# Value-block differences moved from the attention of a batch to the feed-forward of the batch in front, and two late output stores moved two chunks forward

## The chip, the cores and the metric

The kernel runs on one core of a Trainium2 chip. The metric is the time of one execution on the device in microseconds (us); several executions are made and the median is taken. One core has a matrix engine (PE, with its weight loads shown as PEld), a vector engine (DVE), a scalar engine (ACT), a general engine (POOL) and a sync engine (SP). Each works through its own list of instructions in order, and waits for the others through semaphores. DMAs are issued from such a list too: an issue that has to wait, or that takes time itself, holds up whatever stands behind it in the same list. In this kernel nearly all DMAs are issued from SP and POOL.

## The reference

Per batch (8 batches, 3008 tokens, 256 channels, 64 query/key dimensions) a gated attention without softmax, and then a feed-forward over all 24064 tokens:

```python
scores = (z @ z.T) / S                      # 3008 x 3008, symmetric
attn   = relu(scores) ** 2
x      = u * (attn @ v)                     # 3008 x 256
h      = x @ w_in                           # 256 -> 2048
out    = (h * sigmoid(1.702 * h)) @ w_out   # 2048 -> 256
```

Everything is computed in 16-bit floats with 32-bit accumulation; input and output are 32-bit.

## The kernel before, in words

**Tiling.** A batch is cut into 6 chunks of 512 tokens (the last has 448); a chunk has 4 blocks of 128 tokens, so a batch has 24 blocks, the last one half full. Because the score matrix is symmetric, only a part of it is computed: a unit (i, jp) is the pair of key blocks 2jp and 2jp+1 against the queries of chunk i. `scores` (L242) makes it on PE, `relu` (L261) takes it out of PSUM on ACT into one of 3 `rl` buffers, `square` (L270) squares it on DVE into a tile `a`. The mirrored part is made by transposing: `turn_unit` (L326, issue at L331) and two lines of `square` (L287 for the tile `ad` on the diagonal, L308 for `al`) issue DMA transposes from SP. Four of them fill two tiles, `TT[b, i, cj]`.

**Attention of a batch.** Chunks 0, 1, 2 and 5 go through `attend` (L634): per step a few matmuls of value blocks against weights, 24 or 48 steps a chunk, with the gate by `u` on DVE at the end of the chunk (L694). From batch 1 on, chunks 3 (`attend_rows`, L533) and 4 (`attend_split`, L483) are done by Strassen-like products with seven instead of eight parts (P1 to P7). These need sums and differences of the score tiles (`score_forms`, tiles `sa`, L430 to L448) and of the value blocks: `value_forms` (L371) makes four differences for each of three pairs of chunks t = 0, 1, 2, as one or two DVE instructions each (L384), into tiles `vt` of the ring `tt`, which has 14 buffers and is shared with `TT` and with the tiles `gt` of the feed-forward. `still` (L474) hands them to the matmuls of chunks 3 and 4. `VZ` is the half-full last value block, filled by a copy on POOL.

**Order.** All engines' lists are written out by hand. The main loop (L1113) goes over batches, chunks i and steps n; tables keyed by (i, n) say what is slipped in. `fills(b)` (L595) gives the DVE work of chunks 0 to 4: before the change the 12 value forms stand at chunk 0, steps 20 to 43, and chunk 1, steps 14 to 31; the score forms of chunk 3 stand at chunk 1 step 35 to chunk 3 step 18, those of chunk 4 at chunk 3 step 28 to chunk 4 step 23. `sched` says at which steps new units are taken. While chunk 5 runs, the units of chunk 0 of the next batch are made, and their transposes are kept in the list `late`.

**Feed-forward.** `up_group(b, q)` (L717), q = 0 to 47, makes two 128-column groups of `h` on PE (L732), the gelu on ACT (L745, 2 buffers `gf`), and the scaling to `gt` on DVE (L751) or, for q mod 8 in 1, 3, 5, on ACT (L749). The first 16 groups run inside chunk 4, the other 32 after chunk 5, each followed by one part of the second product (`pair_product`, L885; sums of `gt` on DVE, L858 to L871). The last 11 parts (12 for even batches) follow without up groups: the loop over `steps`, L1201, called the tail here. There P7, P3 and P2 are taken out of PSUM by DVE (L922), and P1, P5, P6 by ACT (L920); P7's accumulator is also P4's. From q = 44 on one entry of `late` is issued per step.

**Stores.** `store(b, k)` (L1002) transposes a finished 512-token block `Y[b, k]` on DVE into `yo` (L1007; one buffer) and issues the DMAs to the output from SP (L1017): 4 of 128 KB, or, for the last block of an odd batch, 12 smaller ones, because its last 64 tokens go to another place. Blocks 4 and 5 are not stored in the tail: they wait in `LAST2` and are stored in the attention of the next batch, before the change at chunk 3 step 4 and chunk 4 step 9 (L1144). `Y` has 2 buffers, and the staging tiles `zst` for the next batch's z share them.

**Loads in chunk 4.** At step 4 POOL copies two elements of `TT[b, 4, 5]` into `hold` (L1150), which makes its list wait for the last two transposes of chunk 3, and then issues the loads of the next batch's z (`stage_z`, L160, two halves). `twice_z` (L176) doubles each half on ACT (L179, at steps 19 and 28 of chunk 4) and transposes it from SP (L182). The loads of `u` for chunks 4 and 5 (L214) are on SP too.

Of the kernel before, what the change touches and what calls it, by code (L numbers as in the profile page):

```python
# [10 lines left out]
F16 = mybir.dt.float16  # L11
P = 128
# [3 lines left out]
def kernel(  # L16
# [20 lines left out]
    NJ = (S + P - 1) // P  # L37
# [333 lines left out]
    def value_forms(b, t):  # L371

        def form(f):
            if t not in VT:
                VT[t] = pa.tile([P, 4, CB, P], F16, name="vt", tag="tt", bufs=14)
            (k1, _, _), = key_half(b, t, 0)
            for k2, g, n in key_half(b, t, 1) if f else [(None, 0, CB)]:
                out_, t1, t2 = (VT[t][:, x, g:g + n] for x in (f, 0, 1))
                b11, b12 = k1[:, g:g + n, 0], k1[:, g:g + n, 1]
                a_, b_ = (  # L380
                    (b12, b11) if f == 0 else (k2[:, :, 1], t1) if f == 1
                    else (k2[:, :, 1], b12) if f == 2 else (k2[:, :, 0], t2)
                )
                dve.tensor_tensor(out_, a_, b_, ALU.subtract)  # L384

        return [lambda f=f: form(f) for f in (0, 2, 1, 3)]
# [87 lines left out]
    def still(b, t, g, name):  # L474

        if name in ("P1", "P2", "P3"):
            j = 8 * t + g + (0 if name == "P1" else CB)
            return channels(VZ if j == NJ - 1 else V16[b][:, j], int(name == "P3"))
        return VT[t][:, {"P5": 0, "P6": 1, "P7": 2, "P4": 3}[name], g]

    LAST_SPLIT = (("P2", (2,)), ("P7", (0, 1, 2)), ("P3", (0, 1, 2)), ("P4", (0, 1, 2)))

# [111 lines left out]

    def fills(b):  # L595

        VT.clear()
        SA.clear()
        at = {(0, 19): [lambda: pool.tensor_copy(VZ[TOP], V16[b][TOP, NJ - 1])]}

        def put(i, ns, ops):
            assert len(ns) == len(ops), (i, len(ns), len(ops))
            for n, op in zip(ns, ops):
                at.setdefault((i, n), []).append(op)

        near, far = NCH - 3, NCH - 2
        put(0, (20, 23, 26, 28, 34, 37, 40, 43), value_forms(b, 0) + value_forms(b, 1))
        put(1, (14, 20, 27, 31), value_forms(b, 2))
        put(1, (35, 38, 41, 44), score_forms(b, near, 0))
        put(2, (20, 21, 25, 26, 28, 31, 32), score_forms(b, near, 1, ("S1", "S2", "S3", "S4")))  # L610
        put(2, (38, 39), score_forms(b, near, 2, ("S3",)))
        put(3, (2, 2, 10, 11, 16, 18), score_forms(b, near, 2, ("S1", "S2", "S4")))
        if b < B - 1:
            put(3, (28, 30, 32, 37), score_forms(b, far, 0))
        else:
            put(2, (30, 41), score_forms(b, far, 0, ("S1", "S2")))
            put(3, (28, 30), score_forms(b, far, 0, ("S4", "S3")))
        if b == B - 1:
            put(3, (33, 36), score_forms(b, far, 1, ("S1", "S2")))
            put(4, (3, 5, 7, 9), score_forms(b, far, 2, ("S1", "S2")))  # L620
            put(4, (12, 14), score_forms(b, far, 1, ("S3", "S4")))
            put(4, (17, 19, 21, 23), score_forms(b, far, 2, ("S3", "S4")))
            return at
        put(4, (3, 5), score_forms(b, far, 1, ("S1", "S2")))
        put(4, (9, 10, 12, 13), score_forms(b, far, 2, ("S1", "S2")))
        put(4, (15, 20), score_forms(b, far, 1, ("S4", "S3")))
        put(4, (17, 18, 22, 23), score_forms(b, far, 2, ("S4", "S3")))
        return at
# [434 lines left out]
    LOADL = {(3, 36): 5}  # L1063
    TWICE = {19: 0, 28: 1}

    FIRST_ZT, FIRST_CAST = {12: 4, 20: 5}, {5: 4, 13: 5}
    SCHED0 = {
        0: {2: 1, 6: 2, 14: 2, 22: 2, 30: 2, 38: 2},
# [44 lines left out]
    for b in range(B):  # L1113
        nup = NCH * NFG
        more = b + 1 < B
        sched = SCHED0 if b == 0 else SCHED if more else SCHED_LAST
        turn, load = (TURN, LOAD) if b else (TURN0, LOAD0)
        if split(b, NCH - 2):
            turn, load = (TURNS, LOADS) if more else (TURNL, LOADL)
        head = 0  # L1120
        for i in range(NCH):
            host = b + 1 if more and i == NCH - 1 else b
            if host > b:
                fill(host)
                LATE.append(host)
            if i == 0 and split(b, NCH - 2):
                extra = fills(b)
            for n, step in enumerate(
                attend_split(b, i) if split(b, i) else attend_rows(b, i) if rowed(b, i)
                else attend(b, i, b == 0 and i == 0)  # L1130
            ):
                if b == 0 and i == 0 and n in (5, 24):
                    load_u(0, n // 24)
                if b == 0 and i == 0 and n == 2:
                    copies = first_zt(3)
                if b == 0 and i == 0 and n == 3:
                    copies()
                if b == 0 and i == 0 and n in FIRST_CAST:
                    first_cast(FIRST_CAST[n], True)
                if b == 0 and i == 0 and n in FIRST_ZT:  # L1140
                    first_zt(FIRST_ZT[n])()
                if (i, n) in turn:
                    turn_u(b, turn[i, n])
                if (i, n) in (((3, 4), (4, 9)) if more else ((5, 4), (5, 24))) and LAST2:  # L1144
                    LAST2.pop(0)()
                if (i, n) == (0, 22) and COPY:
                    COPY.pop(0)()
                if split(b, i) and more and n == 4:
                    hold = pw.tile([P, 2], F16, name="hold", tag="hold")
                    pool.tensor_copy(hold, TT[b, i, NCH - 1][:, ::2, 0, 0])  # L1150
                if (i, n) in load:
                    load_u(b, load[i, n])
                if b == 0 and (i, n) in CASTW:
                    cast_w(CASTW[i, n])
                if b == 0 and (i, n) in LOADW:
                    load_w(LOADW[i, n])
                if b == 0 and (i, n) == (NCH - 2, 6):
                    stage_z(1, 0, tag="yo", bufs=1)
                if more and (i, n) == (NCH - 2, 4 if b else 16):
                    load_z(b + 1)  # L1160
                if hosted(b) and i == NCH - 1 and n in LATESUMS:
                    some_sums(NCH * NFG)
                if more and split(b, i) and n in TWICE:
                    twice_z(b + 1, TWICE[n] * NU)
                if b == 0 and i == NCH - 1 and n in (8, 30, 42):
                    wsums.pop(0)()
                take(host, sched[i].get(n, 0))
                if split(b, NCH - 2):
                    for op in extra.get((i, n), ()):
                        op()  # L1170
                if split(b, i):
                    step()
                if i == full(b) and n >= HEAD and (n - HEAD) * LAGY // (2 * NJ - 10) >= head and head < LAGY:
                    up_group(b, head)
                    head += 1
                if not split(b, i):
                    step()
        late.sort(key=lambda t: t[0])
        if more:
            for i in range(2):  # L1180
                load_u(b + 1, i)
            for n0 in range(0, NJ, VB):
                load_v(b + 1, n0)
        prods = products(b)
        for q in range(head, nup):
            if more and q in (head + 14, head + 20):
                k = int(q == head + 20)
                turn_u(b + 1, k)
                load_u(b + 1, k + 2)
            up_group(b, q)  # L1190
            if b == 0 and q == head + 3:
                wsums.pop(0)()
            prods.pop(0)()
            for a_ in AFTER:
                a_[0] -= 1
            while AFTER and AFTER[0][0] < 0:
                AFTER.pop(0)[1]()
            if q >= 44 and late:
                late.pop(0)[1]()
        steps = prods  # L1200
        for step in steps:  # L1201
            step()
            for sum_ in [SUMS.pop(0) for _ in range(min(len(SUMS), 1 + (len(SUMS) > 4)))]:
                sum_[2]()
            for _, turn_it in [late.pop(0) for _ in range(min(len(late), 1 + (len(steps) < 10)))]:
                turn_it()
        LATE.clear()
        if b + 2 == B:
            load_u(b + 1, NCH - 2, "gf")
        if more:  # L1210
            while late:
                late.pop(0)[1]()
            take(b + 1, 2)
# [30 lines left out]
```

## Time and profile before

| | |
|---|---|
| median of 3 executions | 1164.87 us (1164.55 to 1165.69) |
| profiled execution: its own time / span of its instructions | 1164.78 us / 1162.9 us |
| granted PE clock | 1.00 in all 40 slices |
| busy, of the span | PE 99%, DVE 86%, ACT 78%, POOL 15% |
| value forms (L384), 7 batches | 105 DVE instructions, 59.1 us (26.6 + 26.6 + 3.9 + 2.0) |
| store transposes (L1007), all | 46 DVE instructions, 56.2 us |
| DMA issues: store of 128 KB | 156, 2.8 us to landing |
| DMA transposes `tt` / `ad` | 232, 3.4 us / 35, 2.5 us to landing |
| loads of z (192 KB) | 7, 6.3 us to landing |

The attention of batch 1 begins at about 158 us, that of the others at 302, 443, 588, 729, 873 and 1015 us. In batch 2, chunk 0 begins at 302, chunk 1 at 318, chunk 2 at 328, chunk 3 at 338 and chunk 4 at 348 us.

How to read it: busy times are sums over one execution. A timeline line gives the start, the time, the engine, the source line, the operation, what it writes and reads, how many instructions are merged in the line, and in brackets the idle time before it with what ended it. "SPq" and "POOLq" are the lists in which DMAs are issued; the time of an SPq line is the time that issuing took, not the transfer.

### The profile page before, as it was taken

How to read it: one execution, taken by the hardware profiler on the slowest of the kernel's cores; microseconds unless marked ns; L12 is line 12 of the kernel's file. 1: busy time of each engine (PE TensorE's matmuls, PEld its weight loads, DVE VectorE, ACT ScalarE, POOL GpSimd, SP SyncE). 2: the span in 40 equal slices, each digit the busy share in tenths (PEclk: the TensorE clock that was granted, in tenths of full speed). 3: DMA queues.
4: the chain of work that ended last, by engine and by line, in shares of the span. 5: the costliest groups of instructions: out<-in, count | busy, mean ns of one | idle time of the engine just before them, and what ended most of it. 6: DMA issues, size and time to landing. Idle time of an engine off the chain costs nothing.

```text
span 1162.9 us, 22852 instructions
## 1 busy us (share of the span) xinstructions
PE 1156.2 (99%) x8720; PEld 609.7 (52%) x8720; DVE 999.5 (86%) x1736; ACT 907.6 (78%) x1065; POOL 179.1 (15%) x248
## 2 busy tenths in 40 slices
PE   9999999999999999999999999999999999999998
PEld 3544456544465445654446545465444654547446
DVE  7789879998799987999879997899978999698876
ACT  7888867788678886688876887768868688684785
POOL 3033200132001320023100231003110131200000
PEclk9999999999999999999999999999999999999999
DMA  9996399754997559976498765996559874695123
GB/s 225 202 168 98 76 172 163 106 92 88 175 154 104 91 108 175 145 110 88 97 176 145 115 89 106 178 145 109 84 104 175 136 122 81 130 176 91 32 37 74
DMA packets 480543, 143.62 MB, mean 123 GB/s; under 512 B 447664, under 2 KB 476080, under 8 KB 480432
## 3 DMA queue, kind: packets, MB, share of 16 engines
q1 hardware_dynamic: 426272, 108.26, 55.3%
q0 software_dynamic: 52800, 32.58, 18.0%
q8 instruction: 68, 1.11, 0.4%
q10 hardware_dynamic: 1360, 1.31, 0.3%
q14 instruction: 43, 0.35, 0.1%
HBM read 60.29 MB, written 24.64 MB: 73 GB/s over the span
## 4 chain that ended last, share of the span: by engine, by line
PE 97%; DVE 1%; ACT 1%; issue 0%; SPq 0%; DMA 0%; DVEq 0%; ACTq 0%
PE o L677 29%; PE hg L732 27%; PE st L905 23%; PE sc L254 6%; PE oz L499 5%; PE oz L557 5%; PE st L953 1%; PE yp L879 1%; ACT rl L267 0%; PE w L101 0%; DMA uq<-in_u_dram 0%; SPq L308 0%; DVE gt L751 0%; ACT gf L745 0%; DVE yo L1007 0%
## 5 line engine op out<-in xcount | busy, mean ns | idle before, releaser
L745 ACT ACTIVATE gf<-hg 128x1024 f32<-128x1024 f32 (+1 forms) x384 | 382.3, 1003 | 85.9 <-PE hg L732 66.9
L267 ACT ACTIVATE rl<-sc 128x1024 f16<-128x1024 f32 (+1 forms) x344 | 310.6, 940 | 117.7 <-PE sc L254 104.3
L732 PE MATMUL hg<-xt,W 128*128 128x512 f16 (+1 forms) x1408 | 353.4, 374 | 0.1
L677 PE MATMUL o<-a,V 64*128 64x512 f16 (+3 forms) x2078 | 266.8, 368 | 0.3 <-DVE a L298 0.3
L751 DVE TENSOR_SCALAR gt<-gf 128x1024 f16<-128x1024 f32 x282 | 195.0, 694 | 64.0 <-ACT gf L745 61.9
L677 PEld LDWEIGHTS <-V 64*128 64x128 f16 (+1 forms) x3058 | 156.2, 94 | 172.1 <-issue 5.6
L732 PEld LDWEIGHTS <-W 128*128 128x128 f16 x1536 | 149.6, 98 | 156.4 <-issue 3.2
L298 DVE TENSOR_TENSOR a<-rl 128x1024 f16<-128x1024 f16 (+1 forms) x223 | 148.8, 673 | 49.2 <-ACT rl L267 48.6
L214 POOL DMA_DIRECT2D uq<-in_u_dram x120 | 84.7, 717 | 368.1 <-DVE ut L221 170.5
L254 PE MATMUL sc<-ZT 64*128 64x512 f16 (+3 forms) x688 | 117.0, 356 | 0.7 <-ACT ZT L145 0.3
L905 PEld LDWEIGHTS <-WT 128*128 128x128 f16 x736 | 72.0, 98 | 79.7 <-issue 0.9
L749 ACT ACTIVATE gt<-gf 128x1024 f16<-128x1024 f32 (+1 forms) x102 | 104.4, 1024 | 3.6
L677 PE MATMUL o<-tt,V 64*128 64x512 f16 (+1 forms) x766 | 101.7, 376 | 0.0
L905 PE MATMUL st<-gt,W 128*128 128x512 f16 (+1 forms) x368 | 89.9, 370 | 0.0
L905 PE MATMUL st<-s,WT 128*128 128x512 f16 (+1 forms) x368 | 89.3, 370 | 0.0
L905 PE MATMUL st<-gt,WT 128*128 128x512 f16 (+1 forms) x368 | 88.7, 370 | 0.0
L905 PEld LDWEIGHTS <-W 128*128 128x128 f16 x552 | 53.9, 98 | 58.2
L1150 POOL COPY hold<-tt 128x2 f16<-128x2 f16 x6 | 1.6, 270 | 426.2 <-DMA tt<-a 356.1
L922 DVE SCALAR_TENSOR_TENSOR y<-st,y 128x512 f32<-128x512 f32 (+1 forms) x69 | 45.7, 662 | 19.1 <-PE st L905 18.3
L869 DVE TENSOR_TENSOR s<-s,gt 128x1024 f16<-128x1024 f16 (+1 forms) x92 | 60.0, 663 | 0.8
L871 DVE TENSOR_TENSOR s<-gt,s 128x1024 f16<-128x1024 f16 (+1 forms) x92 | 59.3, 661 | 1.3
L867 DVE TENSOR_TENSOR s<-gt 128x1024 f16<-128x1024 f16 (+1 forms) x92 | 59.2, 660 | 0.9
(129 smaller groups left out, 1365.5 us busy)
## 6 DMA issues: line engine op xcount, KB each, us to landing
out_dram<-yo SPq DMA_DIRECT2D x156, 128.0 KB, 2.8
uq<-in_u_dram POOLq DMA_DIRECT2D x116, 128.0 KB, 3.3
V<-in_v_dram POOLq DMA_DIRECT2D x35, 256.0 KB, 6.5
uq<-in_u_dram SPq DMA_DIRECT2D x44, 128.0 KB, 4.4
tt<-a SPq DMA_TRANSPOSE x232, 3.4
uq<-in_u_dram SPq DMA_DIRECT2D x28, 112.0 KB, 3.9
out_dram<-yo SPq DMA_DIRECT2D x28, 96.0 KB, 2.3
wst<-in_moe_w_in_dram POOLq DMA_DIRECT2D x4, 512.0 KB, 5.5
```

The costliest lines, as they stand in the source:

```text
L214: eng.dma_start(uq[k * QW:(k + 1) * QW, :n // QW].rearrange("t q c k -> t q (c k)"), src[:, :, cs])
L254: pe.matmul(sc[:, r, :q1 - q0], zt[h, 2 * kp + r, :], zt[h].rearrange("d n p -> d (n p)")[:, q0:q1], start=True, stop=True,)
L267: act.activation(rl[:, :, :n], sc[:, :, :n], AF.Relu, scale=csc)
L298: dve.tensor_tensor(a[:, :, :n], rl[:, :, :n], rl[:, :, :n], ALU.mult)
L677: ins = pe.matmul(acc[c][:, :n], channels(V16[b][h, j], c), weights(b, i, j)[h], start=(k, m) == first[c], stop=(k, m) == final[c],)
L732: pe.matmul(hg[:, e, :n], W1[:, c, ff * P:(ff + 1) * P], XT[b, i][:, c, :n], start=(c == 0), stop=(c == NCC - 1),)
L745: act.activation(gf[:, :, :n], hg[:, :, :n], AF.Gelu_apprx_sigmoid, scale=1.0 / FSC)
L749: act.activation(g, gf[:, :, :n], AF.Copy, scale=FSC)
L751: dve.tensor_scalar(g, gf[:, :, :n], FSC, None, ALU.mult)
L869: dve.tensor_tensor(s_, ST[b, s, "S1", m], a11, ALU.subtract)
L871: dve.tensor_tensor(s_, a12, ST[b, s, "S2", m], ALU.subtract)
L905: pe.matmul(bank, right[:, ff], lhs[:, f], start=new and ff == 0, stop=ff == NFF // 2 - 1, skip_group_check=True,)
```

## The change

The 12 value forms of batch b+1 are made in the feed-forward of batch b: four after the up groups q = 41, 43, 45 and 47, and eight after steps 3 to 10 of the tail, one each. The tiles are keyed by batch as well, and the copy into `VZ` is issued on POOL ahead of the tail. The entries in chunks 0 and 1 of `fills` are gone. The two stores kept in `LAST2` are made at chunk 0 step 30 and chunk 3 step 4 of the next batch instead of chunk 3 step 4 and chunk 4 step 9. The last batch keeps its places for the stores; batch 0 has none to make. No arithmetic and no matmul changes.

```diff
     def value_forms(b, t):
...
-            if t not in VT:
-                VT[t] = pa.tile([P, 4, CB, P], F16, name="vt", tag="tt", bufs=14)
+            if (b, t) not in VT:
+                VT[b, t] = pa.tile([P, 4, CB, P], F16, name="vt", tag="tt", bufs=14)
...
     def fills(b):
 
-        VT.clear()
         SA.clear()
-        at = {(0, 19): [lambda: pool.tensor_copy(VZ[TOP], V16[b][TOP, NJ - 1])]}
+        at = {}
...
-        put(0, (20, 23, 26, 28, 34, 37, 40, 43), value_forms(b, 0) + value_forms(b, 1))
-        put(1, (14, 20, 27, 31), value_forms(b, 2))
         put(1, (35, 38, 41, 44), score_forms(b, near, 0))
...
+    FORMS, FORMQ = (0, 0, 0, 1, 1, 1, 1, 1, 1, 1, 1, 0, 0), (41,43,45,47)
...
-                if (i, n) in (((3, 4), (4, 9)) if more else ((5, 4), (5, 24))) and LAST2:
+                if (i, n) in (((0, 30), (3, 4)) if more else ((5, 4), (5, 24))) and LAST2:
                     LAST2.pop(0)()
...
         prods = products(b)
+        forms = [form for t in range(NCH // 2) for form in value_forms(b + 1, t)] if more else []
         for q in range(head, nup):
...
             up_group(b, q)
+            if q in FORMQ and more:
+                forms.pop(0)()
...
         steps = prods
-        for step in steps:
+        if more:
+            pool.tensor_copy(VZ[TOP], V16[b + 1][TOP, NJ - 1])
+        for x, step in enumerate(steps):
             step()
+            for form in [forms.pop(0) for _ in range(FORMS[x] if more else 0)]:
+                form()
```

More of the change, by code (lines that the diff above doesn't have):

```diff
@@ L373, in form @@
         def form(f):
-            if t not in VT:
-                VT[t] = pa.tile([P, 4, CB, P], F16, name="vt", tag="tt", bufs=14)
+            if (b, t) not in VT:
+                VT[b, t] = pa.tile([P, 4, CB, P], F16, name="vt", tag="tt", bufs=14)
             (k1, _, _), = key_half(b, t, 0)
             for k2, g, n in key_half(b, t, 1) if f else [(None, 0, CB)]:
-                out_, t1, t2 = (VT[t][:, x, g:g + n] for x in (f, 0, 1))
+                out_, t1, t2 = (VT[b, t][:, x, g:g + n] for x in (f, 0, 1))
                 b11, b12 = k1[:, g:g + n, 0], k1[:, g:g + n, 1]
@@ L478, in still @@
             return channels(VZ if j == NJ - 1 else V16[b][:, j], int(name == "P3"))
-        return VT[t][:, {"P5": 0, "P6": 1, "P7": 2, "P4": 3}[name], g]
+        return VT[b, t][:, {"P5": 0, "P6": 1, "P7": 2, "P4": 3}[name], g]
     LAST_SPLIT = (("P2", (2,)), ("P7", (0, 1, 2)), ("P3", (0, 1, 2)), ("P4", (0, 1, 2)))
```

## The prediction

> **What bounds the kernel now.** First the page: which engine has no room, and whether the chain that ended last runs through it.
>
> ```profile
> span 1162.9 us, 22852 instructions
> PE 1156.2 (99%) x8720; PEld 609.7 (52%) x8720; DVE 999.5 (86%) x1736; ACT 907.6 (78%) x1065; POOL 179.1 (15%) x248
> PEclk9999999999999999999999999999999999999999
> ```
>
> PE is busy for all but 6.7 us, at full granted clock. The table by stretches says where those 6.7 us lie: 2.2 in the first 60 us, 4.4 in the last 13 us, and 0.2 in the 1090 us between. So the change, which touches neither end, has about 0.2 us to win in the open, plus what modelled ends of matmuls hide: the starts of matmuls in PE's timeline are further apart than their pitch by 0.16 to 0.22 us in chunk 4 of batches 1, 5 and 6 (217, 788 and 932 us), 0.5 us together. It can lose far more: whatever makes PE wait comes straight onto the end.
>
> Next, what PE depends on with the least to spare. The timeline of SP's list in batch 6 (chunks 1 to 3):
>
> ```profile
> 893.38 1.24 SPq L287 DMA_TRANSPOSE ad<-a  x1
> 894.71 8.16 SPq L331 DMA_TRANSPOSE tt<-a  x6
> 902.97 1.22 SPq L287 DMA_TRANSPOSE ad<-a  x1
> 904.29 6.22 SPq L331 DMA_TRANSPOSE tt<-a  x4
> ```
>
> Each line starts where the one before ends. This holds from 872 to 910 us, and in every batch from 1 to 6: a transpose takes 1.3 us to issue, and through chunks 0, 1 and 2 SP issues one after another with no idle time. What is put into SP's list there delays all that stands behind it until SP first runs dry, near the end of chunk 2. The DMA engines are full as well:
>
> ```profile
> 873.00:920.00 47.00, 47.00 (x523) 26.56 (x521) 41.38 (x83) 35.84 (x44) 0.00 (x0) 1.00 0.96 166
> ```
>
> (PE busy 47.00 of 47.00 us, DVE 41.38, and last the DMA share 0.96 and 166 GB/s.)
>
> What waits for these transposes: in DVE's timeline at the end of chunk 2 of batch 6
>
> ```profile
> 906.97 0.42 DVE L448 TENSOR_TENSOR sa<-a,sa 128x512 f16<-128x512 f16 x1
> 907.30 0.42 DVE L448 TENSOR_TENSOR sa<-ad,sa 128x512 f16<-128x512 f16 x1
> 907.64 0.75 DVE L446 TENSOR_TENSOR sa<-a 128x512 f16<-128x512 f16 x2
> 909.15 1.29 DVE L694 TENSOR_TENSOR xt<-o,ut 128x512 f16<-128x512 f32 x2 [0.76 <-PE o L677]
> ```
>
> The second L448 reads the `ad` issued at 902.97, which took 4.1 us to land (907.07). Behind it on DVE stands the gate of chunk 2, L694, which frees the accumulators; in batch 2 the gate ends at 339.35 and the first matmul of chunk 3 on a freed bank starts at 339.40. So PE stops as soon as the gate is late.
>
> The second tight place is chunk 4 (batch 2 here; POOL, ACT, SP):
>
> ```profile
> 349.85 0.19 POOL L1150 COPY hold<-tt 128x2 f16<-128x2 f16 x1 [71.74 <-DMA tt<-a]
> 350.48 1.03 POOL L160 DMA_DIRECT2D zst<-in_z_dram  x1 [0.44 <-DVE yr L588]
> ...
> 359.46 0.83 ACT L179 ACTIVATE zst<-zst 128x768 f16<-128x768 f16 x1
> 360.19 0.38 ACT L511 ACTIVATE ya<-oz 128x256 f32<-128x256 f32 x1
> 360.46 1.03 ACT L745 ACTIVATE gf<-hg 128x1024 f32<-128x1024 f32 x1
> ...
> 342.02 2.40 SPq L1017 DMA_DIRECT2D out_dram<-yo  x4
> 344.53 3.27 SPq L331 DMA_TRANSPOSE tt<-a  x2
> 347.90 2.48 SPq L308 DMA_TRANSPOSE al<-a  x2
> 350.56 2.05 SPq L214 DMA_DIRECT2D uq<-in_u_dram  x4
> 356.09 6.77 SPq L1017 DMA_DIRECT2D out_dram<-yo  x12
> ```
>
> `hold` waits for the two transposes at 344.53, which stand right behind a store; the load of z goes out after `hold`, takes 6.9 us (357.4), and ACT doubles it at 359.46, 2.1 us later. Behind that on ACT is the gelu that ends at 361.49; PE's up group that needs its bank starts at 361.56.
>
> **The change part by part.**
>
> *A, the value forms.* 105 instructions on DVE, 59.1 us, 8.4 us a batch, keep their number and size; 15 move per boundary. Back to back they start 0.60 us apart (0.68 long), and the split pairs of t = 2 take 0.47 + 0.22. Four go behind q = 41 to 47: 2.4 us. There DVE's timeline at the end of batch 1 has idle gaps of 1.06 and 1.29 us, both waiting for gelus: 2.35 us. Eight go into the tail: 5 x 0.60 + 3 x 0.69 = 5.1 us, against gaps of 2.23, 0.17 and 0.10 ahead of the three L922 and 2.42 us ahead of the first square of the next batch: 4.9 us. About 0.3 us spills over the boundary; the first square starts at 304.1 instead of 303.76, and gaps of 0.23 and 0.70 us behind it take that back. Its first reader on PE is step 14 of chunk 0, at 306.3, 1.8 us after the square's end. The one tight pair is L922 of P7 and the first matmul of P4 in the same bank: 0.8 us to spare in odd batches (299.69 to 300.45), 0.5 in even ones, and three or four forms ahead of it make it about 0.1 late. Rings: at tail step 3 the ring `tt` holds 8 `gt`, 4 `TT` and 2 `vt`, exactly 14, so no allocation waits for PE; the third `vt` takes a `gt` that P7 has done with. Value 0; bounds 0 and 3.5 us (the tight pair 0.5 late at 7 boundaries). DVE's relief of 8.4 us in chunks 0 and 1 wins nothing on SP, which is full there whatever DVE does, nor on PE, which does not wait. The copy into `VZ` leaves POOL's list in chunk 0 and stands ahead of the tail, where POOL has nothing else: 0.
>
> *B, the store at chunk 0 step 30* (batches 1 to 6). On DVE 1.24 us take the place of 8 forms: 0. On SP 4 issues go in behind unit (1, 6). The price of 4 such issues is in the rows above: 342.02 to 344.53, 2.5 us to the next transpose. Everything behind is 2.5 us later, up to `ad` of chunk 3. What each batch has to spare is the time from the landing of `ad` to the second L448, plus the 0.76 us that DVE is idle ahead of the gate: batch 1: 188.50 + 2.5 to 191.83, 0.8 + 0.76 = 1.6; batches 2, 3, 4: 336.21, 477.52 and 621.65 against landings at 333.9, 475.3, 619.1, so 2.9 or more; batch 5: 761.3 to 762.96, 2.35; batch 6: 907.07 to 907.30, 1.0. Late by 0.9, 0, 0, 0, 0.15 and 1.5: 2.5 us on PE. Bounds: 0, if the stall of one load (the 4.1 us landing in batch 6, where 2.5 is usual) does not come back and DVE gains a little; and 8.8 us, with 3.85 us for the store, which is 2.5 plus the extra issue time of the transposes behind it in batch 1 (200.15: 3.24 for two and 3.34 for two `al`, against 1.3 each).
>
> *C, the store at chunk 3 step 4.* There it was block 4, 4 issues; now it is block 5. After an even batch that is again 4 issues. After an odd batch (stores in batches 2, 4, 6) it is 12: 6.77, 6.72 and 6.34 us against 2.40, 3.11 and 2.42 for the four, so the two transposes that `hold` waits for go out 4.4, 3.6 and 3.9 us later, and the z load with them. ACT's doubling had 2.1, 2.35 and 2.8 us to spare (landings 6.9, 6.6 and 5.8 us after 350.48, 636.00 and 922.19; doubling at 359.46, 644.90, 930.80). ACT then stands for 2.3, 1.2 and 1.1 us, and PE behind it with 0.1 us of room: 4.6 us. What B leaves over in SP's list adds up to 0.5 us in batch 2, and the transposes behind the store may issue 0.6 us faster than the 3.27 and 3.15 seen; I leave both out. Bounds: 1 us (z lands in 5.8 us each time, and 0.6 us comes back) and 7 us (B's delay reaches `hold` whole).
>
> *D, chunk 4 step 9 without its store.* DVE has 1.24 us more room, and ACT's waits for L751 (0.68 to 0.92 us) shrink. Nearly all of it is hidden behind PE; the visible part is the 0.5 us above: −0.5, bounds −0.5 and 0. The second half of z, held back by the store until 356.61, can go out with the first; its doubling has room already.
>
> Sum: 0 + 2.5 + 4.6 − 0.5 = +6.6 us. On the profiled execution's own 1164.78 us, which lies 0.09 under the median of the runs shown, that is 1171.4, and as a median 1171.5 us (+0.57%).
>
> **The rivals.** No change to be measured here means within 0.2%, 2.3 us.
>
> *The store costs DMA time, not issue time.* Speaks for it: DMA share 0.96 at 166 GB/s over these chunks, so 0.5 MB more means 3.2 us, and landings of 4.1 instead of 2.5 us occur. Against: between loads the transposes keep their 1.3 us. B becomes (3.2 less 1.6, 2.9, 2.9, 3.3, 2.35, 1.0) 1.6 + 0.3 + 0.3 + 0.85 + 2.2 = 5.2, and what is left over moves C to 6: with a little of A's bound, 1164.9 + 12 = 1177. The Trainium skill, "DMA: Bandwidth & Descriptors", section "Issuing engines are not separate DMA queues", says that DMAs from any engine's list share the same 16 DMA engines and interleave; by that rule it is this time, and the trace's DMA share agrees with it, while the steady 1.3 us of issue speaks for the list.
>
> *The delays are swallowed.* SP's list runs dry at 338.8 in batch 2 for 2 us; if the displaced issues find such room earlier, because the squares come sooner from a freer DVE, B is 0, and if z's load lands faster without stores beside it, C is 1 or 2. Then 1164.5 to 1167, say 1165.5. Against: no idle time stands in SP's rows before the end of chunk 2.
>
> *Faster.* Chunk 4 is the place: ACT waits 0.68 to 0.92 us for DVE there, the store's 1.24 us being what DVE was late with. If PE's busy time hides such waits at 0.7 us in each of 6 batches, 1164.9 − 4.2 = 1160.7. It decides if up groups of chunk 4 start later than their pitch by 0.4 us a batch or more; the timeline shows 0.2 at most. The Trainium skill, "Perfetto Trace Analysis", section "Identifying the Most-Contended Engine", warns that matmul busy time says little about how near PE is to its peak; here the start-to-start pitch, 0.21 us for 512 columns, agrees with the busy time.
>
> *DVE becomes the bound in the tail.* If the forms wait for something (a `vt` for its buffer) L922 of P7 comes late by more than 0.5 us: 7 x 0.8 = 5.6 us more, 1177. Against: the count of 14.
>
> **How the numbers follow.** The forecast 0.56, DMA time 0.10, DVE in the tail 0.05, swallowed 0.23, faster 0.06. Swallowed is "same", except for a tenth; of the forecast nearly all is slower. So faster 0.06, same 0.23, slower 0.71. The range leaves out the faster case and the upper part of the heavy ones: 1164.6 to 1177.5; the forecast's own range, from the bounds of B and C, is 1167 to 1176.
>
> **What would show it.** In the profile after: the vt lines (L384) behind L751 and L922 at the end of each batch, with the gap of 2.4 us ahead of the first square gone; SP's list with 4 stores between two L331 in chunk 0 and transposes some 2.5 us later; in batches 1 and 6 the second L448 idle on a DMA and the gate late, with a start-to-start gap on PE at the start of chunk 3; in batches 2, 4 and 6 twelve issues ahead of `hold`, and ACT L179 idle on zst for 1 to 2 us. PE's idle time, 6.7 us now, would be 12 to 14. The prediction is wrong if L179 does not wait, if SP's list shows room in chunk 1, or if PE waits in the tail.

## The result and the profile after

The changed kernel takes 1179.44 us (median of 4, 1177.25 to 1182.09), against 1164.98 for the kernel before (1164.55 to 1165.69): 1.0125 times, 95% interval 1.0113 to 1.0138. It is slower by 14.5 us. The forecast was slower by 6.6 us, with a range that ended at 1177.5.

The profiled execution took 1178.86 us. Its page, the first lines and the chain that ended last:

```profile
span 1177.1 us, 22849 instructions
PE 1161.8 (99%) x8720; PEld 609.8 (52%) x8720; DVE 999.8 (85%) x1736; ACT 907.8 (77%) x1065; POOL 178.4 (15%) x248
PEclk9999999999999999999999999999999999999999
...
PE 87%; DMA 5%; DVE 4%; ACT 2%; issue 2%; SPq 0%; DVEq 0%; POOL 0%; ACTq 0%; POOLq 0%
```

The number of matmuls is the same and PE is still "99%" busy, so its share says little. PE's idle time went from 6.7 to 15.3 us, and another 5.6 us appear as busy time: matmuls that wait among one another are counted as busy here, and some ran slowly (below). A matmul-by-matmul comparison shows it better. Take the start of each of the 8720 matmuls in turn, subtract the start of the same one in the kernel before, and see where this difference grows:

| PE's loss in us, profiled executions | chunk 2 | chunk 3 | chunk 4 | elsewhere |
|---|---|---|---|---|
| batch 1 | 0.92 | 1.80 | −0.25 | 0 |
| batch 2 | 0 | 1.06 | 1.29 | 0.1 |
| batch 3 | 0.13 | 1.48 | 0 | 0 |
| batch 4 | 0 | 1.06 | 0.72 | 0 |
| batch 5 | 0 | 1.29 | −0.22 | 0 |
| batch 6 | 0 | 0.39 | 4.05 | −0.2 |
| all, with batch 7 | 1.05 | 7.2 | 5.6 | −0.1 |

The waits that are new in the table of waits of the changed kernel (in total, times, longest) name the three places:

```profile
DVE sa L442 <- DMA tt<-a: 9.5, 10, 2.2
DVE sa L448 <- DMA ad<-a: 5.7, 7, 1.3
ACT zst L179 <- DMA zst<-in_z_dram: 5.0, 3, 3.1
PE oz L499 <- ACT ya L511: 3.9, 3, 2.7
```

**The score forms of chunk 3.** The timeline of SP's list in batch 6, which has the store of chunk 0 in it:

```profile
896.95 2.61 SPq L1014 DMA_DIRECT2D out_dram<-yo  x4
899.66 4.80 SPq L331 DMA_TRANSPOSE tt<-a  x3
904.55 1.22 SPq L287 DMA_TRANSPOSE ad<-a  x1
905.93 8.14 SPq L331 DMA_TRANSPOSE tt<-a  x6
914.17 2.22 SPq L287 DMA_TRANSPOSE ad<-a  x1
```

Four store issues take 2.7 us to the next transpose, as the prediction had it. But the three transposes behind them take 4.80 us. In the kernel before six take 8.26 us to the next row, 1.38 us each from start to start, so three take 4.05: the transposes are held up as well. DVE's timeline at the end of chunk 2, in batch 2 and in batch 6, and in batch 5 at the start of chunk 3:

```profile
339.04 0.42 DVE L448 TENSOR_TENSOR sa<-a,sa 128x512 f16<-128x512 f16 x1
340.69 0.43 DVE L448 TENSOR_TENSOR sa<-ad,sa 128x512 f16<-128x512 f16 x1 [1.23 <-DMA ad<-a]
341.03 0.75 DVE L446 TENSOR_TENSOR sa<-a 128x512 f16<-128x512 f16 x2
341.70 1.28 DVE L691 TENSOR_TENSOR xt<-o,ut 128x512 f16<-128x512 f32 x2
...
776.17 0.76 DVE L442 TENSOR_TENSOR sa<-a,tt 128x512 f16<-128x512 f16 x2 [1.44 <-DMA tt<-a]
...
918.04 0.42 DVE L448 TENSOR_TENSOR sa<-ad,sa 128x512 f16<-128x512 f16 x1 [1.17 <-DMA ad<-a]
```

The second L448 now waits for `ad`, and the idle 0.76 us ahead of the gate (L691, L694 before the change) are used up. That is the prediction's first tight place, but in batch 2, where it expected no loss; in batch 6, where it expected the largest, PE loses 0.39 us. The line of batch 5 is a place that the prediction did not have: the first score form of chunk 3 itself, behind the gate, waits for two transposes.

**The load of z.** Batch 2, from the timelines of POOL, ACT and SP:

```profile
357.31 0.66 POOL L1148 COPY hold<-tt 128x2 f16<-128x2 f16 x1 [76.65 <-DMA tt<-a]
357.91 2.54 POOL L160 DMA_DIRECT2D zst<-in_z_dram  x2
...
364.40 0.84 ACT L179 ACTIVATE zst<-zst 128x768 f16<-128x768 f16 x1 [1.25 <-DMA zst<-in_z_dram]
...
345.60 6.94 SPq L1014 DMA_DIRECT2D out_dram<-yo  x12
352.65 2.61 SPq L331 DMA_TRANSPOSE tt<-a  x2
```

Twelve store issues, then the two transposes, then `hold`, then z, which lands as ACT begins to double it; ACT idles for it. This is the prediction's step C.

**A stretch at half speed.** In batch 6 ACT's idle time before L179 is 3.1 us, and PE pauses for 2.73 us. The table by stretches there. Behind the length of the stretch stand the busy times of PE, PEld, DVE, ACT and POOL, with the number of instructions, and then the granted clock, the DMA share and GB/s:

```profile
940.00:942.00 2.00, 2.00 (x12) 1.02 (x11) 1.59 (x4) 0.51 (x1) 0.36 (x1) 1.00 1.66 167
942.00:944.00 2.00, 0.05 (x1) 0.00 (x0) 0.00 (x0) 0.39 (x1) 0.00 (x0) 1.00 2.95 107
944.00:946.00 2.00, 1.22 (x6) 0.86 (x6) 0.33 (x1) 2.00 (x5) 0.00 (x0) 0.55 0.25 34
946.00:948.00 2.00, 2.00 (x10) 0.91 (x8) 2.00 (x5) 0.96 (x2) 0.00 (x0) 0.60 1.10 213
948.00:950.00 2.00, 2.00 (x15) 1.26 (x13) 1.32 (x3) 1.72 (x2) 0.00 (x0) 1.00 1.02 179
```

The granted clock goes from 1.00 to 0.50 at 944.18 us, while PE still stands, and back at 947.59; the 0.55 and 0.60 are means over stretches that hold both. PE works from 944.78 on, so 2.81 us of its work run at half speed and 1.4 us are lost. 2.73 + 1.4 is 0.1 more than the 4.05 us that batch 6 loses in chunk 4.

### The profile page after: what moved, and what is told of

Same layout as the page of the kernel before. It is cut to its first block, busy times and chain, and to the rows that moved or that the text cites. A ratio compares the mean times of both kernels' runs of the same rounds, so it can differ in the third digit from the quotient of the medians.

```text
span 1177.1 us, 22849 instructions
## 1 busy us (share of the span) xinstructions
PE 1161.8 (99%) x8720; PEld 609.8 (52%) x8720; DVE 999.8 (85%) x1736; ACT 907.8 (77%) x1065; POOL 178.4 (15%) x248
## 3 DMA queue, kind: packets, MB, share of 16 engines
q8 instruction: 68, 1.11, 0.4%
## 4 chain that ended last, share of the span: by engine, by line
PE 87%; DMA 5%; DVE 4%; ACT 2%; issue 2%; SPq 0%; DVEq 0%; POOL 0%; ACTq 0%; POOLq 0%
PE hg L729 26%; PE o L674 24%; PE st L902 23%; PE sc L254 5%; PE oz L499 5%; DMA tt<-a 3%; PE oz L557 2%; DMA zst<-in_z_dram 1%; PE st L950 1%; ACT rl L267 1%; DMA ad<-a 1%; PE yp L876 1%; DVE sa L448 0%; DVE sa L442 0%; DVE sa L444 0%
## 5 line engine op out<-in xcount | busy, mean ns | idle before, releaser
L859 DVE TENSOR_TENSOR gt<-gt 128x1024 f16<-128x1024 f16 (+1 forms) x92 | 58.3, 652 | 0.0
```

## The experiments

The theory after the result: nothing comes from the value forms; about 8 us come from the store in chunk 0, through transposes that come later than its issues alone would make them; about 6 us come from the 12 issues ahead of `hold`. Its rivals: the forms in the tail cost something after all; the store costs list time alone; the two stores cost more together than apart.

**The forms alone.** The changed kernel with the stores at their old places:

```diff
-                if (i, n) in (((0, 30), (3, 4)) if more else ((5, 4), (5, 24))) and LAST2:
+                if (i, n) in (((3, 4), (4, 9)) if more else ((5, 4), (5, 24))) and LAST2:
```

> The value forms moved as in the change, both stores at their old places (chunk 3 step 4, chunk 4 step 9). Theory (the stores' places in SP's list cost the time): nothing changes, 1164.2 to 1166.0 us, and matmul by matmul PE runs as before. Rival (forms in the tail push DVE's work over the batch boundary and PE pays): 1168 us or more, with PE waits at the start of chunk 0.

Measured: 1164.48 us (10 runs), 0.9997 times (0.9988 to 1.0007). Moving 59 us of DVE work out of the attention neither wins nor loses. So the 14.5 us come with the stores.

**The stores alone.** The kernel before with the stores at the new places:

```diff
-                if (i, n) in (((3, 4), (4, 9)) if more else ((5, 4), (5, 24))) and LAST2:
+                if (i, n) in (((0, 30), (3, 4)) if more else ((5, 4), (5, 24))) and LAST2:
```

> Only the two stores moved, the value forms stay in chunks 0 and 1. Theory (SP's list): the whole loss, 1177 to 1182 us, since SP is full in chunks 0 to 2 whatever DVE does. Rival (the two edits cost only together): under 1172 us.

Measured: 1181.52 us (4 runs), 1.0152 times (1.0126 to 1.0178). The interval meets that of the whole change, so the times do not tell the two apart. The matmuls of the profiled execution, with 1174.41 us the shortest of the four, do: PE loses 0.42 us at the end of chunk 0 in each of batches 1 to 6, 2.5 us together, and in the changed kernel nothing. In DVE's timeline of this kernel the transpose of the store stands among the forms of chunk 0 with no gap up to the gate:

```profile
314.87 1.24 DVE L1007 STREAM_TRANSPOSE yo<-y 128x1024 f32<-128x1024 f32 x1
316.03 0.65 DVE L298 TENSOR_TENSOR a<-rl 128x1024 f16<-128x1024 f16 x1
316.60 0.68 DVE L384 TENSOR_TENSOR vt<-V 128x512 f16<-128x512 f16 x1
...
321.15 1.28 DVE L694 TENSOR_TENSOR xt<-o,ut 128x512 f16<-128x512 f32 x2
```

So with the forms in place the store costs DVE's time in chunk 0 as well, 2.5 us in all. Moving the forms makes room for that, but most of the price is not paid on DVE.

**Each store alone.** First, the changed kernel with only the first store at its new place, so that its second store is block 5 at chunk 4 step 9:

```diff
-                if (i, n) in (((0, 30), (3, 4)) if more else ((5, 4), (5, 24))) and LAST2:
+                if (i, n) in (((0, 30), (4, 9)) if more else ((5, 4), (5, 24))) and LAST2:
```

> The change, but with the second store back at chunk 4 step 9: only the first one is early (chunk 0 step 30). Theory: the losses of chunks 2 and 3 stay (1.05 + 7.2 us in the changed kernel's trace), those of chunk 4 go: 1171.5 to 1174.5 us. Rival (the twelve issues ahead of the z load are the main cost): under 1169 us.

Measured: 1172.8 us (4 runs, 1171.57 to 1177.44), 1.0074 times (1.005 to 1.0097): +7.9. In the profiled execution, the shortest of the four, PE loses 2.5 us in chunk 2 and 4.9 in chunk 3.

Then the other store alone, by the old places and the old transposes in chunk 0, but with block 5 (12 issues in even batches) ahead of block 4:

```diff
-                if (i, n) in (((0, 30), (3, 4)) if more else ((5, 4), (5, 24))) and LAST2:
-                    LAST2.pop(0)()
+                if (i, n) in (((3, 4), (4, 9)) if more else ((5, 4), (5, 24))) and LAST2:
+                    LAST2.pop(-1 if more else 0)()
```

> Forms moved, stores at the old places but in the other order: block 5 at chunk 3 step 4 and block 4 at chunk 4 step 9, so that only the twelve issues ahead of the two transposes that the z load waits for are left of the change. Theory: PE loses in chunk 4 of batches 2, 4 and 6 alone, 0.7 to 2.3 us each, 1167.0 to 1170.0 us, with ACT L179 waiting for zst in these batches. Rival (z is late only with what the first store has left over in SP's list): 1164.5 to 1165.8 us.

Measured: 1169.08 us (7 runs), 1.0032 times (1.0021 to 1.0043): +4.1. PE loses only in chunk 4: 0.41, 1.01 and 1.78 us in batches 2, 4 and 6, and 0.6 in batch 5, whose cause stays open. ACT waits for z at L179 in batches 4 and 6 alone (0.52 and 1.64 us), not in batch 2 as expected. 7.9 and 4.1 make 12.0; the whole change has 14.5. In the profiled execution 1.4 us of the rest are the half-speed stretch, which this kernel does not have: its longest pause of PE in chunk 4 is 1.57 us, and the granted clock stays at 1.00 behind it. But one such stretch lowers the mean granted clock by 0.0015, and the longest execution of the changed kernel, 1182.09 us, has a mean of 1.000. So the stretch does not explain the median, and most of the 2.5 us stay open.

**The load of z without its wait.** The last kernel, with the one edit that `hold` reads a constant in place of the two transposes:

```diff
-                    pool.tensor_copy(hold, TT[b, i, NCH - 1][:, ::2, 0, 0])
+                    pool.tensor_copy(hold, ident[:, :2])
```

> As the run with block 5 stored first, but POOL's small copy ahead of the z load reads a constant instead of the two transposes behind the twelve issues, so the z load does not wait for them. Theory (late z is what PE pays for): the 4 us go, 1164.2 to 1166 us, and ACT L179 waits for nothing. Rival (the twelve issues cost through the u loads or the transposes behind them): 1167 to 1169.5 us, PE late in chunk 4 as before.

Measured: 1165.5 us (10 runs), 1.0005 times (0.9995 to 1.0015). 0.6 us are left of the 4.1, which the interval does not tell from nothing, with the same 12 issues at the same place. In the profiled executions the 1.78 us of batch 6 become 0.05 and the 1.01 of batch 4 0.39; but batch 2 keeps its loss (0.39 for 0.41), which therefore was not the late z. The same edit in the changed kernel:

> The changed kernel, its two stores at chunk 0, step 30 and at chunk 3, step 4, with the one edit that POOL's `hold` copy of chunk 4 reads a constant instead of the two transposes; the copy's own time stays. If everything that the changed kernel loses in chunk 4 is the late z load behind that wait, with the half-speed stretch of TensorE that follows its 2.7 us pause in batch 6, then what is left is the cost of the store in chunk 0 alone, as the kernel with that store alone has shown it: 1172 to 1174 us, 1.006 to 1.008 times the kernel before. If the two stores together load the queues and DMA engines so that more is lost than by each alone, it stays above 1175. The rows to look at: matmuls of chunk 4 after the z load, and the granted clock around 945 us, which should be 1.00 if no pause there is longer than 2 us.

Measured: 1174.28 us (4 runs, 1172.88 to 1178.69), 1.0094 times (1.0073 to 1.0116). The wait of `hold` is worth 1179.4 − 1174.3 = 5.2 us in the changed kernel. In batch 2 its timelines (POOL, ACT) now read

```profile
349.17 0.27 POOL L1148 COPY hold<-ident 128x2 f16<-128x2 f16 x1 [69.17 <-PE sc L254]
349.80 2.12 POOL L160 DMA_DIRECT2D zst<-in_z_dram  x2 [0.36 <-ACT yr L580]
...
361.63 0.83 ACT L179 ACTIVATE zst<-zst 128x768 f16<-128x768 f16 x1
```

z goes out 8 us earlier and ACT waits for nothing at L179. No pause of PE is longer than 0.9 us from batch 1 to the end of batch 7's attention, and chunk 4 loses nothing. What is left, 9.6 us, is a little more than the first store alone (7.9), with intervals that overlap; whether the two stores load each other beyond `hold` and the half-speed stretch stays open.

**What the store in chunk 0 costs with.** Two reasons were left for its price: the time of SP's list, which the prediction took, and its bytes on DMA engines that are full, which was a rival there. The remaining kernels are all the one with the first store alone, changed in the store of block 4 of batches 0 to 5.

A quarter of the bytes with all four issues (the other three quarters of these rows are not stored):

```diff
+                n_ //= part
                 sp.dma_start(
                     out[r:r + n_].rearrange("(q t) c -> t q c", t=QW)[:, :, cs],
```

> As the run with only the first store early, with its 4 issues on SP, but each carries a quarter of the tokens (three quarters of block 4 of batches 0 to 5 are never stored): SP's issues without most of the bytes. Issue theory: SP's list is still 2 us or more later, 1169 to 1173 us. DMA theory: 1165 to 1168 us.

Measured: 1167.09 us (10 runs), 1.0016 times (1.0006 to 1.0025): +2.2 in place of +7.9, as expected of a price that is paid in bytes.

All the bytes, in runs of the same size, with one issue (the runs go to permuted places inside the block's rows):

```diff
+            sp.dma_start(
+                out[r:r + n_].rearrange("(q t) (cb x) -> (t cb) q x", t=QW, cb=P // QW),
+                yo[:, :n_ // QW].rearrange("p q c k -> p q (c k)"),
+            )
+            return
```

> The changed kernel with its first store at chunk 0, step 30 and its second at chunk 4, step 9, and in batches 0 to 5 the store of block 4 is one DMA issue in place of four: the same 512 KB from all 128 partitions, in the same 2048 runs of 256 bytes, but the runs go to permuted places inside the block's 512 rows of the output, so these rows hold the right values in the wrong order. If the cost is SP's time for issuing, which was my step's, SP's list is held up by one issue of about half a us in place of 2.5 us, under every allowance of that step (the smallest was 1.0): 1165 to 1166 us. If the cost is the bytes on the DMA engines, the transposes behind the store still come some 2.5 to 3.5 us later than in the kernel before, the first of them takes 3 us or more to issue in place of 1.3, and the time stays at 1169 to 1173 us.

Measured: 1169.25 us (7 runs, 1167.12 to 1171.57), 1.0035 times (1.0023 to 1.0046): +4.4. The time is in the range that the bytes alone were to give, at its lower end, but the rows are not: 2.04 us of issues less save 3.5 us, and 4.4 remain. SP's list behind the store, in batch 2, shows it for each kernel. The kernel before, where no store stands there:

```profile
309.70 11.64 SPq L331 DMA_TRANSPOSE tt<-a  x8
321.44 1.22 SPq L287 DMA_TRANSPOSE ad<-a  x1
```

The first store alone, whole:

```profile
318.99 2.56 SPq L1014 DMA_DIRECT2D out_dram<-yo  x4
321.65 5.25 SPq L331 DMA_TRANSPOSE tt<-a  x3
326.99 1.23 SPq L287 DMA_TRANSPOSE ad<-a  x1
```

A quarter of the bytes, four issues:

```profile
318.19 1.96 SPq L1015 DMA_DIRECT2D out_dram<-yo  x4
320.24 4.53 SPq L331 DMA_TRANSPOSE tt<-a  x3
324.87 1.22 SPq L287 DMA_TRANSPOSE ad<-a  x1
```

All the bytes, one issue:

```profile
321.48 0.53 SPq L1013 DMA_DIRECT2D out_dram<-yo  x1
322.10 5.83 SPq L331 DMA_TRANSPOSE tt<-a  x3
328.02 1.24 SPq L287 DMA_TRANSPOSE ad<-a  x1
```

Count the last row of each against that of the kernel before, less what batch 1 had already lost (2.19, 1.39 and 4.65 us at the first matmul of batch 2): `ad` is issued 3.4, 2.0 and 1.9 us later. The store's issues are 2.66, 2.05 and 0.62 us of that, start to next start, and the three transposes behind them take 1.2, 0.5 and 1.8 us longer than 4.05. In the kernel before the eight took 0.7 us longer than their pitch of 1.38 us, and that part is not paid again; with it the sums agree with the 3.4, 2.0 and 1.9 us to 0.2. One batch alone carries this only roughly: in the forms alone, where no store stands there, the same `ad` comes between 0.8 us earlier and 1.1 us later than in the kernel before. Over batches 1 to 6 the means are 3.5, 2.4 and 2.3 us, in the same order, and 0.2 in the forms alone. So the price has two parts. The list is held for the time of the issues; and then the next transposes take longer to issue, less so with a quarter of the bytes (0.5 us in place of 1.2). One issue in place of four takes 2.04 us off the first part and adds 0.6 to the second.

The one-issue kernel's profiled execution loses 5.0 of its 6.9 us of chunk 3 in batch 1, where one `ad`, issued at 190.51, lands 5.4 us later. DVE waits for it:

```profile
196.01 0.42 DVE L448 TENSOR_TENSOR sa<-ad,sa 128x512 f16<-128x512 f16 x1 [3.33 <-DMA ad<-a]
```

Up to 1.7 of the 5.0 us are a half-speed stretch behind the pause. Why this one transpose took so long is not known, and not every execution has it: the mean granted clock is 0.998 in the two longest of the seven, the profiled one among them, and 1.000 in three of the others (1167.12, 1167.36 and 1169.62 us). In batches 2 to 6 the one issue loses 1.9 us in chunk 3, the quarter of the bytes 1.8, and the whole store with four issues 5.3 in chunks 2 and 3.

The same four issues, but from POOL's list:

```diff
-                sp.dma_start(
+                eng.dma_start(
```

> As the run with only the first store early, but its 4 DMAs are issued from POOL instead of SP: the same bytes at the same time on the same DMA engines, without SP's issues. Issue theory (SP's list is what is full): chunks 2 and 3 lose next to nothing, 1164.2 to 1167 us. DMA theory (0.5 MB more on full DMA engines, about 3 us): the loss stays, 1171 to 1174 us.

Measured: 1187.08 us (4 runs, 1182.53 to 1189.49), 1.0185 times (1.0158 to 1.0212): worse by 14.3 us than from SP. Neither of the two expectations holds. Batch 2 in the timelines of POOL, SP and PE:

```profile
318.61 2.57 POOL L1014 DMA_DIRECT2D out_dram<-yo  x4 [35.80 <-DVE yo L1004]
...
315.09 15.73 SPq L331 DMA_TRANSPOSE tt<-a  x8
330.92 1.23 SPq L287 DMA_TRANSPOSE ad<-a  x1
...
327.31 1.04 PE L674 MATMUL o<-tt,V 64*128 64x512 f16 x8 [2.31 <-DMA tt<-a]
```

SP has no store in its list, and yet its eight transposes take 15.73 us against 11.64: they are issued into the middle of the store's transfer. One of them, issued 2.0 us behind the first store DMA, takes 4.6 us to issue and 7.8 to land. With SP issuing, the store goes in front, and the three transposes behind it landed in 3.2 to 4.4 us in this batch. So here PE waits at once, in chunk 1, in five batches, for 2.0 to 4.5 us each. Part of the price is the clock: the profiled execution (1189.49 us) has four stretches at half speed, up to 1.7 us each, and that of the first store alone has none; but the shortest execution, 1182.53 us, with a mean granted clock of 0.999 against 0.994, is still 9.7 us above the first store alone. And the edit changes more than the list. On the page the store leaves the queue hardware_dynamic, where it was 2112 packets, for software_dynamic, where it is 192. Whether the place in the midst of the transposes or the other queue makes it dearer is not separated.

The Trainium skill, "DMA: Bandwidth & Descriptors", section "Issuing engines are not separate DMA queues", says that DMAs from all lists run on the same 16 engines and interleave, so that another issuing engine saves only the time of issuing. The trace agrees with the first part (15.73 us with no issue of a store in the list). For the second, saving 2.66 us of issues on SP came out 14.3 us dearer.

## Why the prediction was wrong in size

The sign was right, and PE waited at the two places that the prediction had named. By the table of the profiled execution, B cost 5.7 us more than forecast and C 1.5 more. By its steps:

*A, the value forms, 0.* Right: 0.9997 by itself, and no loss outside chunks 2 to 4. In the changed kernel's timeline the forms fill the gap ahead of the first square, which comes some 0.3 us later in its batch, as worked out.

*B, the store in chunk 0, +2.5.* This is the step that failed: 7.9 us measured alone, 8.2 by the table of the changed kernel. The mis-sized term is the price of four issues, "2.5 us to the next transpose". Issues do take that, but it left out what the transposes behind them lose, 0.8 to 1.2 us more. The prediction had seen this: its upper bound took 3.85 us from batch 1 of the kernel before, where transposes behind a store took longer, and came to 8.8 us. That was the row to take, since there as here several transposes stand behind the store: with 3.5 us, the mean over the batches of the first store alone, in place of 2.5, the prediction's own allowances give 7.0 us. Even the row beside the one taken showed it: the two transposes behind the store of batch 2 took 3.27 us, where the pitch gives 2.67. How steep it is beyond the allowances can be read off the runs roughly: at a mean displacement of 2.3 to 2.4 us 2.2 us are lost (a quarter of the bytes) or 4.4 (one issue, with the one slow landing), at 3.5 us 7.9.

The split over the batches was wrong too. 1.5 of the 2.5 us were to come from batch 6, where the `ad` of chunk 3 took 4.1 us to land. That landing belonged to one execution: in the forms alone the same `ad` lands in 2.51 us. In the changed kernel it comes only 1.7 us later in its batch (914.17 − 902.97 − 9.5), and PE loses 0.39 us.

The allowances were also too generous. In the changed kernel the first `ad` of chunk 3 comes 3.4 to 3.8 us later in batches 2 to 4, against an allowance of 2.9; that would lose 0.5 to 0.9 us, and 1.06 to 1.61 were lost. They were counted to the second L448 alone. The wait at the score forms with L442 (9.5 us in total, the largest of the new waits on DVE) was not among them; in batch 2 it stands 3 us ahead of that L448, and in the odd batches also behind the gate.

*C, the store at chunk 3 step 4, +4.6.* The mechanism is right: 4.1 us alone, all but 0.6 gone when `hold` does not wait; 5.2 in the changed kernel with it. Its sizes by batch were off, so that the sum comes near is in part luck: alone, 0.41, 1.01 and 1.78 us were lost where 2.3, 1.2 and 1.1 were forecast, and the 0.41 was not the late z. Batch 2 lost 1.29 us in place of 2.3: z was issued 7.43 us later (357.91 against 350.48), of which 2.56 is the delay at the start of the batch and 1.06 what chunk 3 lost, so that ACT came later too; it landed in 6.46 us in place of 6.85; and 7.43 − 2.56 − 1.06 − 0.39 − 2.1 of room makes 1.3. Batch 4 goes the same way (0.72 in place of 1.2). Batch 6 lost 4.05 in place of 1.1. z was issued 4.4 us later by the same count, 0.5 more than the 3.9 assumed, and took 7.15 us to land in place of 5.78: 4.4 + 1.4 − 2.8 = 3.0, and ACT stood idle for 3.1 us ahead of L179. Then came 1.4 us of half speed, which no step had.

*D, −0.5.* The number is right, −0.25 and −0.22 us in batches 1 and 5, with batch 6 hidden in the loss. The reason is not shown: the first store alone, which still has a store at chunk 4 step 9, gains the same −0.25 and −0.21, and the forms alone, with both stores at their old places, the −0.25. So this is luck.

Of the rivals, "the store costs DMA time" with 1177 us came nearest, and it had 1 in 10. Its B of 5.2 us was too small also, as it counted the bytes in place of the issues, and both are paid. "Swallowed" fell because SP has no idle time before the end of chunk 2, "faster" because chunk 4 had only half a us to give, and "DVE in the tail" by the forms alone.

No run beat the kernel before by more than the noise. With PE idle for 0.2 us in the 1090 us between the two ends, and 0.5 us in the pitch of chunk 4, no place for these stores could win more than 0.7 us, which 0.2% does not show.

## What to carry to other kernels

A DMA that was put into a full list between others cost twice here: its issues held the list, and the issues behind it took longer, the more bytes it had. Take the price from a row with the same neighbours, and count to where the list is back on its pitch, not to the next issue. When something in order is moved later, list every consumer to the next idle stretch with its allowance, the ones behind the first stalled consumer too. And making room on one engine (59 us of DVE work here, worth nothing by itself) does not pay for work whose price is paid in another queue.

## What the runs showed of the hardware that I had not expected

A pause of PE can cost more than itself. Within the kernels the granted clock fell to 0.50 six times, for 3.41 us each: once in the changed kernel (from 944.18 us, with a pause of 2.73 us), four times in the store by POOL (from 179.81, 473.36, 766.90 and 934.15) and once in the one-issue kernel (from 198.83, behind a pause of 2.20 us). The first three of the store by POOL came with pauses of 2.96, 3.30 and 4.51 us; pauses of 1.11, 1.57, 2.05 and 2.31 us brought none. The table by stretches of the store by POOL, for the pause at 176.04 and for the fourth:

```profile
176.00:178.00 2.00, 0.04 (x2) 0.09 (x1) 0.00 (x0) 1.30 (x2) 0.00 (x0) 1.00 1.10 211
178.00:180.00 2.00, 0.99 (x10) 0.54 (x12) 0.00 (x0) 0.00 (x0) 0.00 (x0) 0.95 1.23 258
180.00:182.00 2.00, 2.00 (x12) 0.86 (x10) 0.32 (x1) 1.38 (x2) 0.00 (x0) 0.50 0.98 184
182.00:184.00 2.00, 2.00 (x16) 0.98 (x14) 2.00 (x3) 1.62 (x2) 0.00 (x0) 0.69 0.98 187
...
932.00:934.00 2.00, 1.48 (x17) 0.70 (x12) 2.00 (x5) 1.02 (x1) 0.00 (x0) 1.00 1.05 195
934.00:936.00 2.00, 1.81 (x16) 1.48 (x17) 1.41 (x4) 0.38 (x1) 0.00 (x0) 0.54 0.97 182
```

The half speed begins 0.6 us before PE takes up work again in the changed kernel, and 0.6 to 1.1 us after it behind the three long pauses of the store by POOL. In batch 1 of that kernel, 2.96 us of pause became a loss of 4.81.

The length of the pause is not the whole condition: ahead of 934.15 no pause is longer than 0.66 us. The starts in the store by POOL lie 86, 86 and 49 times 3.413 us apart. Divide each of the eleven traces into windows of 3.413 us on the grid of its own clock changes, and count the matmuls that start in each window, in units of 128 rows by 512 columns (two of 64 rows, or two of 256 columns, are one unit; at the pitch of 0.21 us, 16 fit). The six windows ahead of a half-speed stretch hold 3 to 5.25 units. No other window up to the last matmuls of a kernel holds fewer than 6: the pause of 1.57 us left 6 units in its window, that of 2.05 us 6, that of 2.31 us 7. So in these runs what counted was how little work fell into one window, and it depends on where the window starts as well as on the pause. The margin, 5.25 against 6, is thin, and no experiment was made on it.

The Trainium skill, "TensorE: Matmul & The Clock Gate", section "Part 1: The HAM clock gate", describes a clock that is either full or half, and halved after a window of about 3.4 us without work, whose start does not follow the kernel. The clock of 0.50, the 3.41 us and the grid agree. That pauses of 2.73 and 2.96 us were enough, shorter than that window, and windows with up to 5.25 units of work in them, is not what it says.
